# Softplus in an attention and dense-layer chain: where one plus the exponential is added

## The chip, the cores and the metric

The kernel runs on one core of a Trainium2 chip. The metric is the device time of one execution in microseconds (us). The engines are named as the profile names them: PE (TensorE, matmuls; PEld its weight loads), DVE (VectorE), ACT (ScalarE), POOL (GpSimd) and SP (SyncE, which issues most transfers).

## The reference

Windowed attention over q, k, v gives x of 1536 tokens by 512. A gated layer follows, then a layer with softplus:

```python
a = x @ w1
b = x @ w2
h = a * b @ w3
x = h @ w_out                                   # 1536 x 512
h = x @ w_in                                    # 1536 x 2048
g = np.maximum(h, 0.0) + np.log1p(np.exp(-np.abs(h)))
return g @ w_out2                               # 1536 x 512
```

`w_in` and the last `w_out` belong to the last dense part, in which the change lies. All values are float32.

## The kernel before

Every large matrix product is made with three matmuls: each operand is split into a high part and the remainder, a low part, and `mm3` (lines 164 to 168) adds high x high, high x low and low x high in PSUM. So each product of a 128x128 stationary block with a 128x512 moving block stands as three matmuls, at lines 166, 167 and 168.

The program goes through banded attention, two stages that make the gated products (`ab`) and the product of the two later weights (`w34`), a third that gives y, and then `stage4`, the last dense part (lines 724 to 783). It is built of 48 steps: three chunks t of 512 tokens, and in each 16 blocks f of 128 of the 2048 hidden columns.

- A step makes `h` of its block: 12 matmuls into one PSUM bank (tag S, 4 buffers).
- `softplus` (lines 688 to 722), a generator in three parts, turns `h` into `g`. Part one: the absolute value (L704, ACT), the exponential of its negative (L705, ACT) into tile `spa`, and one plus that into tile `spu` (L706, POOL). Part two: the logarithm of it into `spl` (L709, ACT), then three DVE operations (L711, L714, L717), of which the first two correct for the rounding of the sum and add the positive part of `h`. Part three: the high part `gh` (L720, ACT cast) and the low part `gl` (L151, DVE subtraction).
- `outs` adds `g` of a block times the output weights: 12 matmuls into four accumulators, `ox` and `o`, for four groups of 128 tokens. Here slices of `gh` and `gl` are the stationary operand.

The generator is driven so that `h` of a step is followed by part one of the same step, part three of the step before, then part two of the same step. `outs` runs two steps behind `h`. In the last two steps it is held back; then come the outputs of blocks 12, 13 and 14, and block 15 in pieces. The very last softplus works in two halves of 256 columns, into the tile `glast`, so that its first half can be used early.

For the first chunk a scheduler orders each engine's instructions from its own costs; for the other two the order is that of the code (`manual_schedule`). In the first chunk, at f = 3, 5, 7 and 9, `w4_unit` also decodes weight units 12 to 15, which arrive as 64-bit words. Each unit is two halves, and each half takes on ACT L193 and L196 (`dt`) and the cast to the high part `w4h` (L226), on DVE L201, L204, L210 and L215 and the subtraction for the low part `w4l` (L151). Units 0 to 11 were decoded earlier. Line 196 has a bias from a tile of one value per partition (`rebias`, line 912).

Of the kernel before, what the change touches and what calls it, by code (L numbers as in the profile page):

```python
# [9 lines left out]
F32 = mybir.dt.float32  # L10
# [6 lines left out]
ALU = mybir.AluOpType  # L17
AF = mybir.ActivationFunctionType
PSUM = bass.MemoryType.PSUM

P = 128
# [38 lines left out]
    P=(-697.11, -455.77, -631.6, -474.64, -647.58, -395.71), PV=(97.88, 94.31, 94.22, 97.88, 97.88, 169.98),  # L60
# [81 lines left out]
class Net:  # L142
# [545 lines left out]
    def softplus(self, pool, ps, f, t, parts=1):  # L688

        nc = self.nc  # L690

        def tl(n, dt=F32, nb=2):
            return pool.tile([P, CH], dt, tag=n, name=f"{n}{t}_{f}", bufs=nb)

        a, u, l = tl("spa"), tl("spu"), tl("spl")
        if (t, f) == (NCH - 1, NF2 - 1):

            g = self.slot(SLOT_AB, "glast")
            gh, gl = g[:, 0, :], g[:, 1, :]
        else:  # L700
            gh, gl = tl("gh", FR, 3), tl("gl", FR, 3)
        cuts = [slice(j * CH // parts, (j + 1) * CH // parts) for j in range(parts)]
        for c in cuts:
            nc.scalar.activation(a[:, c], ps[:, c], AF.Abs)  # L704
            nc.scalar.activation(a[:, c], a[:, c], AF.Exp, scale=-1.0)  # L705
            nc.gpsimd.tensor_scalar(out=u[:, c], in0=a[:, c], scalar1=1.0, scalar2=1.0, op0=ALU.add, op1=ALU.mult)  # L706
        yield
        for c in cuts:
            nc.scalar.activation(l[:, c], u[:, c], AF.Ln)  # L709

            nc.vector.scalar_tensor_tensor(  # L711
                out=u[:, c], in0=u[:, c], scalar=1.0, in1=a[:, c], op0=ALU.subtract, op1=ALU.subtract
            )
            nc.vector.scalar_tensor_tensor(  # L714
                out=u[:, c], in0=ps[:, c], scalar=0.0, in1=u[:, c], op0=ALU.max, op1=ALU.subtract
            )
            nc.vector.tensor_tensor(out=l[:, c], in0=l[:, c], in1=u[:, c], op=ALU.add)  # L717
        yield
        for c in cuts:
            self.last_hi = nc.scalar.copy(gh[:, c], l[:, c])  # L720
            self.lo_dve(gl[:, c], l[:, c], gh[:, c])
        yield gh, gl
# [184 lines left out]
    def run(self):  # L907
        tc, nc = self.tc, self.nc
        with tc.tile_pool(name="const", bufs=1) as const:
            self.flag = const.tile([P, 1], I32, name="flag")  # L910
            self.val = const.tile([P, 2], F32, name="val")
            self.rebias = const.tile([P, 1], F32, name="rebias")
            self.idle = const.tile([P, P], BF, name="idle")
            nc.vector.memset(self.idle, 0.0)
            nc.vector.memset(self.rebias, -8.0 * 16 * 896)
            nc.scalar.preload_act_table_set("natural_log_exp_and_others")
            self.bad = None
            self.net(True)
            with tc.If(self.bad != 0):
                self.net(False)  # L920
# [48 lines left out]
```

## Time and profile before

| | |
|---|---|
| runs of the kernel | 584.95 us median of 3 (584.88 to 585.05) |
| the profiled execution | 584.81 us, of which 582.9 us are its span |
| granted PE clock | 0.998 of full speed over the span |
| PE busy | 573.5 us, 98% |
| PE weight loads busy | 472.8 us, 81% |
| DVE busy | 431.0 us, 74% |
| ACT busy | 347.1 us, 60% |
| POOL busy | 82.4 us, 14% |

The span runs from the first to the last instruction that the profile records. Busy shares are means over stages with different limits: a share says what an engine does, not who waits for it. Matmuls overlap in the pipeline, so the distance between the starts of two of them, not the length of one, tells the pace of PE. In a timeline the bracket at a row's end is the engine's idle time ahead of that instruction and what ended it.

### The profile page before, as it was taken

How to read it: one execution, taken by the hardware profiler on the slowest of the kernel's cores; microseconds unless marked ns; L12 is line 12 of the kernel's file. 1: busy time of each engine (PE TensorE's matmuls, PEld its weight loads, DVE VectorE, ACT ScalarE, POOL GpSimd, SP SyncE). 2: the span in 40 equal slices, each digit the busy share in tenths (PEclk: the TensorE clock that was granted, in tenths of full speed). 3: DMA queues.
4: the chain of work that ended last, by engine and by line, in shares of the span. 5: the costliest groups of instructions: out<-in, count | busy, mean ns of one | idle time of the engine just before them, and what ended most of it. 6: DMA issues, size and time to landing. Idle time of an engine off the chain costs nothing.

```text
span 582.9 us, 9844 instructions
## 1 busy us (share of the span) xinstructions
PE 573.5 (98%) x3718; PEld 472.8 (81%) x3718; DVE 431.0 (74%) x906; ACT 347.1 (60%) x712; POOL 82.4 (14%) x162
## 2 busy tenths in 40 slices
PE   9999999999999999999999999999999999999996
PEld 6888788888888888888888777888888888888885
DVE  6889899999989976767988889845644554654553
ACT  7999967667566754545666668544444344444352
POOL 4657700000000000000000221111111011011010
PEclk9999999999999999999999999999999999999999
DMA  7566645454445523342643221000200000200002
GB/s 275 172 221 195 188 140 149 139 151 151 133 144 148 164 88 108 114 140 72 201 128 106 74 72 37 0 1 0 73 0 2 0 1 1 73 0 1 0 1 79
DMA packets 15512, 54.51 MB, mean 94 GB/s; under 512 B 1888, under 2 KB 1888, under 8 KB 15456
## 3 DMA queue, kind: packets, MB, share of 16 engines
q1 hardware_dynamic: 15168, 53.27, 29.3%
q8 instruction: 31, 0.51, 0.4%
q10 hardware_dynamic: 288, 0.52, 0.3%
q14 instruction: 25, 0.20, 0.1%
HBM read 50.64 MB, written 3.15 MB: 92 GB/s over the span
## 4 chain that ended last, share of the span: by engine, by line
PE 86%; POOL 4%; DVE 3%; ACT 3%; issue 2%; DMA 1%; SPq 0%; POOLq 0%; DVEq 0%
PE ab L166 8%; PE ab L168 7%; PE ab L167 7%; PE h L167 6%; PE h L168 6%; PE h L166 6%; PE x2p L168 4%; PE x2p L166 4%; PE x2p L167 4%; PE ox L168 3%; PE o L167 3%; PE o L168 3%; PE o L166 3%; PE ox L167 3%; PE ox L166 3%; PE w34p L168 2%
## 5 line engine op out<-in xcount | busy, mean ns | idle before, releaser
L706 POOL TENSOR_SCALAR spu<-spa 128x512 f32<-128x512 f32 (+1 forms) x49 | 35.9, 733 | 458.7 <-ACT spa L705 458.7
L151 DVE TENSOR_TENSOR gl<-spl,gh 128x512 fp32r<-128x512 f32 x47 | 32.6, 694 | 76.8 <-ACT gh L720 76.5
L704 ACT ACTIVATE spa<-h 128x512 f32<-128x512 f32 (+1 forms) x49 | 28.7, 586 | 86.5 <-PE h L168 86.3
L166 PE MATMUL ab<-x,u_w 128*128 128x512 f32 x192 | 74.8, 390 | 0.0
L167 PE MATMUL ab<-x,u_w 128*128 128x512 f32 x192 | 74.7, 389 | 0.0
L168 PE MATMUL ab<-x,u_w 128*128 128x512 f32 x192 | 74.7, 389 | 0.0
L166 PE MATMUL h<-y,w4h 128*128 128x512 f32 x192 | 74.7, 389 | 0.0
L167 PE MATMUL h<-y,w4h 128*128 128x512 f32 x192 | 74.7, 389 | 0.0
L168 PE MATMUL h<-y,w4l 128*128 128x512 f32 x192 | 74.7, 389 | 0.0
L193 ACT ACTIVATE dt_w<-raw_w 128x512 bf16<-128x512 bf16 x64 | 42.5, 669 | 52.1 <-DMA raw_w<-w4d 16.9
L201 DVE SCALAR_TENSOR_TENSOR dc_w<-raw_w,dt_w 128x512 uint16<-128x512 uint16 x64 | 44.2, 697 | 10.1 <-ACT dt_w L196 9.6
L196 ACT ACTIVATE dt_w<-dt_w,rebias 128x512 uint16<-128x512 uint16 x64 | 45.8, 721 | 1.3
L711 DVE SCALAR_TENSOR_TENSOR spu<-spu,spa 128x512 f32<-128x512 f32 (+1 forms) x49 | 33.3, 680 | 16.6 <-ACT spl L709 16.6
L709 ACT ACTIVATE spl<-spu 128x512 f32<-128x512 f32 (+1 forms) x49 | 30.4, 623 | 24.5 <-POOL spu L706 24.5
L407 POOL TENSOR_SCALAR e<-e,st 128x196 f32<-128x196 f32 (+1 forms) x96 | 39.5, 434 | 23.4 <-ACT e L393 17.1
L393 ACT ACTIVATE e<-e,st 128x196 f32<-128x196 f32 (+1 forms) x96 | 42.2, 447 | 0.9 <-DVE st L386 0.7
L168 PEld LDWEIGHTS ab<-x,u_w 128*128 128x128 f32 x192 | 36.1, 188 | 7.5
L167 PEld LDWEIGHTS h<-y,w4h 128*128 128x128 f32 x192 | 36.1, 188 | 7.5
L167 PEld LDWEIGHTS ab<-x,u_w 128*128 128x128 f32 x192 | 36.0, 188 | 7.5
L166 PEld LDWEIGHTS h<-y,w4h 128*128 128x128 f32 x192 | 36.0, 188 | 7.5
L166 PEld LDWEIGHTS ab<-x,u_w 128*128 128x128 f32 x192 | 36.0, 188 | 7.4
L168 PEld LDWEIGHTS h<-y,w4l 128*128 128x128 f32 x192 | 36.0, 188 | 7.4
(127 smaller groups left out, 1306.4 us busy)
## 6 DMA issues: line engine op xcount, KB each, us to landing
raw_w<-w4d SPq DMA_DIRECT2D x32, 511.8 KB, 4.2
raw_w<-w SPq DMA_DIRECT2D x16, 511.8 KB, 4.6
raw_w<-w3t SPq DMA_DIRECT2D x16, 511.8 KB, 3.8
qk<-qk SPq DMA_DIRECT2D x7, 792.0 KB, 4.5
raw_wo<-wod SPq DMA_DIRECT2D x8, 511.8 KB, 3.8
v<-vu SPq DMA_DIRECT2D x8, 400.0 KB, 5.5
v<-v SPq DMA_DIRECT2D x8, 384.0 KB, 4.6
out<-os SPq DMA_DIRECT2D x10, 256.0 KB, 2.3
```

Of the source, the lines that this page charges most:

```text
L151: return engine.tensor_tensor(out=lo, in0=x, in1=hi.bitcast(F32), op=ALU.subtract)
L166: nc.tensor.matmul(ps, lhs[0], rhs[0], start=start, stop=False)
L167: nc.tensor.matmul(ps, lhs[0], rhs[1], start=False, stop=False)
L168: nc.tensor.matmul(ps, lhs[1], rhs[0], start=False, stop=stop)
L193: return nc.scalar.activation(t.bitcast(BF), x["top"].bitcast(BF), AF.Abs)
L196: return nc.scalar.activation(x["t"], x["t"], AF.Relu, bias=self.rebias[:, 0:1], scale=8.0)
L201: nc.vector.scalar_tensor_tensor(out=c, in0=x["top"], scalar=0x8000, in1=t, op0=ALU.bitwise_and, op1=ALU.bitwise_or)
L393: nc.scalar.activation(e, e, AF.Exp, bias=st[:, 0, i : i + 1], scale=-1.0, accum_out=st[:, 1, i : i + 1])
L407: nc.gpsimd.tensor_scalar(out=e, in0=e, scalar1=buf("st", h)[:, 2, i : i + 1], scalar2=1.0, op0=ALU.mult, op1=ALU.mult)
L706: nc.gpsimd.tensor_scalar(out=u[:, c], in0=a[:, c], scalar1=1.0, scalar2=1.0, op0=ALU.add, op1=ALU.mult)
L709: nc.scalar.activation(l[:, c], u[:, c], AF.Ln)
L711: nc.vector.scalar_tensor_tensor(out=u[:, c], in0=u[:, c], scalar=1.0, in1=a[:, c], op0=ALU.subtract, op1=ALU.subtract)
```

## The change

The addition at L706 is made by ACT, as an Identity activation whose bias is a tile that holds one, in all 49 places (47 steps of 512 columns, and the two halves of 256 of the last step). The tile `one` is added and filled by DVE at the start.

```diff
         for c in cuts:
             nc.scalar.activation(a[:, c], ps[:, c], AF.Abs)
             nc.scalar.activation(a[:, c], a[:, c], AF.Exp, scale=-1.0)
-            nc.gpsimd.tensor_scalar(out=u[:, c], in0=a[:, c], scalar1=1.0, scalar2=1.0, op0=ALU.add, op1=ALU.mult)
+            nc.scalar.activation(u[:, c], a[:, c], AF.Identity, bias=self.one[:, 0:1])
...
             self.rebias = const.tile([P, 1], F32, name="rebias")
+            self.one = const.tile([P, 1], F32, name="one")
             self.idle = const.tile([P, P], BF, name="idle")
             nc.vector.memset(self.idle, 0.0)
             nc.vector.memset(self.rebias, -8.0 * 16 * 896)
+            nc.vector.memset(self.one, 1.0)
```

The order of the built program moves in three places. The names carry the chunk and the step: `spa0_3` is tile `spa` of chunk 0, step 3; the last number is a running one.

ACT before, in chunk 0, from the second pass over weight unit 12 to the absolute value of step 4:

```order
L196 ACTIVATE dt_w4_12_1_3863<-dt_w4_12_1_3863,rebias_60 128x512 [waits Activation_49]
L720 CAST gh0_2_3819<-spl0_2_3818 128x512 [waits DVE_49]
L704 ACTIVATE spa0_3_3887<-h0_3_3874 128x512 [waits PE_49]
L705 ACTIVATE spa0_3_3887<-spa0_3_3887 128x512 [waits Activation_49]
L709 ACTIVATE spl0_3_3889<-spu0_3_3888 128x512 [waits Pool_49]
L226 CAST w4h12_3846<-dr_w4_12_0_3856 128x512 [waits DVE_49]
L226 CAST w4h12_3846<-dr_w4_12_1_3869 128x512 [waits DVE_49]
L704 ACTIVATE spa0_4_3926<-h0_4_3913 128x512 [waits PE_49]
```

The same place in the changed program:

```order
L196 ACTIVATE dt_w4_12_1_3865<-dt_w4_12_1_3865,rebias_60 128x512 [waits Activation_49]
L704 ACTIVATE spa0_3_3889<-h0_3_3876 128x512 [waits PE_49]
L720 CAST gh0_2_3821<-spl0_2_3820 128x512 [waits DVE_49]
L705 ACTIVATE spa0_3_3889<-spa0_3_3889 128x512 [waits Activation_49]
L706 ACTIVATE spu0_3_3890<-spa0_3_3889,one_61 128x512 [waits Activation_49]
L709 ACTIVATE spl0_3_3891<-spu0_3_3890 128x512 [waits Activation_49]
L226 CAST w4h12_3848<-dr_w4_12_0_3858 128x512 [waits DVE_49]
L226 CAST w4h12_3848<-dr_w4_12_1_3871 128x512 [waits DVE_49]
L704 ACTIVATE spa0_4_3928<-h0_4_3915 128x512 [waits PE_49]
```

The wait of the logarithm for POOL is gone, the Identity stands in its place, and the absolute value of step 3 has moved ahead of the cast of `gh` of step 2.

PE before, at the first output matmuls of the part (chunk 0, block 0):

```order
L166 MATMUL h0_3_3874<-y0_0_3216,w4h3_3340 128x512 [waits DVE_49]
L167 MATMUL h0_3_3874<-y0_0_3216,w4h3_3340 128x512
L166 MATMUL ox0_0_3830<-w4h0_3328,gh0_0_3767 128x512 [waits PE_49,Activation_49]
L167 MATMUL ox0_0_3830<-w4l0_3329,gh0_0_3767 128x512
L166 MATMUL ox0_1_3831<-w4h0_3328,gh0_0_3767 128x512 [waits PE_49]
L168 MATMUL ox0_0_3830<-w4h0_3328,gl0_0_3768 128x512 [waits DVE_49]
```

PE in the changed program, same place:

```order
L166 MATMUL h0_3_3876<-y0_0_3218,w4h3_3342 128x512 [waits DVE_49]
L167 MATMUL h0_3_3876<-y0_0_3218,w4h3_3342 128x512
L168 MATMUL h0_3_3876<-y0_0_3218,w4l3_3343 128x512
L166 MATMUL ox0_0_3832<-w4h0_3330,gh0_0_3769 128x512 [waits PE_49,Activation_49]
L167 MATMUL ox0_0_3832<-w4l0_3331,gh0_0_3769 128x512
L166 MATMUL ox0_1_3833<-w4h0_3330,gh0_0_3769 128x512 [waits PE_49]
L168 MATMUL ox0_0_3832<-w4h0_3330,gl0_0_3770 128x512 [waits DVE_49]
```

The third matmul of `h` of step 3 has moved from behind the 12 output matmuls to ahead of them.

ACT before, at the end of the part (chunk 2, steps 13 to 15):

```order
L720 CAST gh2_13_5656<-spl2_13_5655 128x512 [waits DVE_49]
L709 ACTIVATE spl2_14_5694<-spu2_14_5693 128x512 [waits Pool_49]
L704 ACTIVATE spa2_15_5719<-h2_15_5706 128x256 [waits PE_49]
L705 ACTIVATE spa2_15_5719<-spa2_15_5719 128x256 [waits Activation_49]
L704 ACTIVATE spa2_15_5719<-h2_15_5706 128x256
L705 ACTIVATE spa2_15_5719<-spa2_15_5719 128x256 [waits Activation_49]
L720 CAST gh2_14_5695<-spl2_14_5694 128x512 [waits DVE_49]
L709 ACTIVATE spl2_15_5721<-spu2_15_5720 128x256 [waits Pool_49] x2
```

And in the changed program:

```order
L706 ACTIVATE spu2_14_5695<-spa2_14_5694,one_61 128x512 [waits Activation_49]
L720 CAST gh2_13_5658<-spl2_13_5657 128x512 [waits DVE_49]
L709 ACTIVATE spl2_14_5696<-spu2_14_5695 128x512 [waits Activation_49]
L704 ACTIVATE spa2_15_5721<-h2_15_5708 128x256 [waits PE_49]
L705 ACTIVATE spa2_15_5721<-spa2_15_5721 128x256 [waits Activation_49]
L706 ACTIVATE spu2_15_5722<-spa2_15_5721,one_61 128x256 [waits Activation_49]
L704 ACTIVATE spa2_15_5721<-h2_15_5708 128x256
L705 ACTIVATE spa2_15_5721<-spa2_15_5721 128x256 [waits Activation_49]
L706 ACTIVATE spu2_15_5722<-spa2_15_5721,one_61 128x256 [waits Activation_49]
L720 CAST gh2_14_5697<-spl2_14_5696 128x512 [waits DVE_49]
L709 ACTIVATE spl2_15_5723<-spu2_15_5722 128x256
```

Three Identity activations now stand on ACT ahead of the cast of `gh` of step 14, where POOL did that work beside it. The order on DVE and SP is unchanged, but for the added fill at the start.

## Rows read from the trace of the kernel before

**Rows 1.** Busy time by stretch (window, engine busy us and count, clock, DMA, GB/s).
```profile
340.00:362.00 22.00, 20.98 (x89) 16.12 (x88) 19.98 (x35) 14.90 (x27) 5.33 (x4) 1.00 0.21 73
```

**Rows 2.** Timeline of PE: start, length, instruction; first, 232nd, last matmul of the part.
```profile
313.57 0.39 PE L166 MATMUL h<-y,w4h 128*128 128x512 f32 x1
...
368.69 0.39 PE L166 MATMUL ox<-w4h,gh 128*128 128x512 f32 x1
...
577.22 0.39 PE L168 MATMUL o<-w4h,glast 128*128 128x512 f32 x1
```

**Rows 3.** Waits of weight loads from 313 us (total, times, longest); the first one's timeline row.
```profile
PEld ox L168 <- DVE gl L151: 2.4, 5, 1.0
...
322.42 0.19 PEld L166 LDWEIGHTS ox<-w4h,gh 128*128 128x128 f32 x1 [0.50 <-ACT gh L720]
```

**Rows 4.** Timeline of ACT, POOL and DVE, chunk 0, steps 3 and 5.
```profile
328.82 0.63 ACT L705 ACTIVATE spa<-spa 128x512 f32<-128x512 f32 x1
329.53 3.12 POOL L706 TENSOR_SCALAR spu<-spa 128x512 f32<-128x512 f32 x1 [5.30 <-ACT spa L705]
331.48 0.69 DVE L151 TENSOR_TENSOR gl<-spl,gh 128x512 fp32r<-128x512 f32 x1
332.69 0.63 ACT L709 ACTIVATE spl<-spu 128x512 f32<-128x512 f32 x1 [3.24 <-POOL spu L706]
333.86 1.29 DVE L151 TENSOR_TENSOR w4l<-dr_w,w4h 128x512 fp32r<-128x512 f32 x2 [1.69 <-ACT w4h L226]
...
341.96 3.05 POOL L706 TENSOR_SCALAR spu<-spa 128x512 f32<-128x512 f32 x1 [5.72 <-ACT spa L705]
```

**Rows 5.** Instructions that write tile spu: ns minimum, median, maximum; first and last start.
```profile
L706 POOL TENSOR_SCALAR spu<-spa x49: 403/617/3122, 317.8 to 568.4; 128x512 f32<-128x512 f32 x47, 128x256 f32<-128x256 f32 x2
```

**Rows 6.** Timeline of DVE: one operation of the decode of units 13, 14 and 15.
```profile
341.04 0.29 DVE L204 TENSOR_SCALAR dt_w<-dc_w 128x512 uint16<-128x512 uint16 x1
...
353.39 0.29 DVE L204 TENSOR_SCALAR dt_w<-dc_w 128x512 uint16<-128x512 uint16 x1
...
364.38 0.29 DVE L204 TENSOR_SCALAR dt_w<-dc_w 128x512 uint16<-128x512 uint16 x1
```

**Rows 7.** ACT by line and shape: count, busy us, mean ns, idle ahead and its releasers.
```profile
L196 ACT ACTIVATE dt_w<-dt_w,rebias 128x512 uint16<-128x512 uint16 x64 | 45.8, 721 | 1.3
L193 ACT ACTIVATE dt_w<-raw_w 128x512 bf16<-128x512 bf16 x64 | 42.5, 669 | 52.1 <-DMA raw_w<-w4d 16.9 <-DVE dr_w L210 11.3 <-DMA raw_w<-w3t 6.3
...
L709 ACT ACTIVATE spl<-spu 128x512 f32<-128x512 f32 x47 | 29.7, 632 | 24.5 <-POOL spu L706 24.5
L705 ACT ACTIVATE spa<-spa 128x512 f32<-128x512 f32 x47 | 29.7, 632 | 1.5
L720 ACT CAST gh<-spl 128x512 fp32r<-128x512 f32 x47 | 28.6, 608 | 12.8 <-DVE spl L717 12.8
L704 ACT ACTIVATE spa<-h 128x512 f32<-128x512 f32 x47 | 28.0, 595 | 86.4 <-PE h L168 86.3
...
L226 ACT CAST w4h<-dr_w 128x512 fp32r<-128x512 f32 x8 | 4.7, 614 | 1.0 <-DVE dr_w L215 1.0
...
L705 ACT ACTIVATE spa<-spa 128x256 f32<-128x256 f32 x2 | 0.8, 418 | 0.1
```

**Rows 8.** Timeline, chunk 2: low part of step 13, and the first matmul that uses step 13.
```profile
565.85 0.69 DVE L151 TENSOR_TENSOR gl<-spl,gh 128x512 fp32r<-128x512 f32 x1 [2.44 <-ACT gh L720]
...
569.29 0.39 PE L166 MATMUL ox<-w4h,gh 128*128 128x512 f32 x1
```

**Rows 9.** Timeline of the tail: ACT, DVE, and the weight load for the first low part.
```profile
568.88 0.62 ACT L720 CAST gh<-spl 128x512 fp32r<-128x512 f32 x1 [0.56 <-DVE spl L717]
569.41 0.72 ACT L709 ACTIVATE spl<-spu 128x256 f32<-128x256 f32 x2
...
572.73 0.42 DVE L151 TENSOR_TENSOR glast<-spl,glast 128x256 fp32r<-128x256 f32 x1
...
573.60 0.19 PEld L168 LDWEIGHTS ox<-w4h,glast 128*128 128x128 f32 x1
```

## The prediction

> **What bounds the kernel now.** I began with the busy time by stretch [rows 1]: between 340 and 362 us TensorE (PE) is busy for 20.98 us of 22, VectorE (DVE) for 19.98, ScalarE (ACT) for 14.90 and GpSimd (POOL) for 5.33. PE is the bound almost everywhere, so only a hole in PE's stream can give time back. The next view is the timeline of PE [rows 2]. The last dense part runs 48 steps of 12 matmuls `h` and 12 matmuls of the output, 1152 in all. The first starts at 313.57, the 232nd at 368.69, the last at 577.22. The last 920 pitches take 208.53 us, 0.2267 us each, with no room for a wait of visible size. The 231 pitches ahead would take 52.37 us at that pace and take 55.12. So **2.75 us** is lost in the whole part, all of it between 313.57 and 368.69, while the last four weight units (12 to 15) are decoded beside the first chunk's steps.
>
> Who made PE wait stands in the waits of its weight loads [rows 3], since here `gh` and `gl` are the stationary operands: `gl` from DVE five times. The first wait of all, at 322.42, is for the first `gh` from ACT; with the short stumbles behind it (up to 323.80, where the 44th matmul would have stood at 323.32) it costs 0.48 us. The other 2.27 us come from 344 us on. There I read ACT, DVE and POOL against each other [rows 4]: the POOL operation of step 3 starts at 329.53 and lasts 3.12 us. The exponential ahead of it ended at 329.45 (328.82 + 0.63). The logarithm behind it (L709) starts at 332.69, after ACT sat idle for 3.24 us. ACT's two casts of weight unit 12 are queued behind that logarithm, and DVE, done with `gl` at 332.17, waits 1.69 us for them and starts its subtraction only at 333.86. At 341.96 the same happens with 3.05 us. The median L706 is 617 ns, the longest 3122 [rows 5]. DVE's own start-to-start distance between decodes shows the effect [rows 6]: 12.35 us from unit 13 to unit 14 (353.39 − 341.04), 10.99 to unit 15 (364.38 − 353.39), against 48 x 0.2267 = 10.88 us that PE needs for two steps. The holes of PE are that delay, arriving a few steps later.
>
> A long POOL span may be an artefact. **A rule against my reading:** the Trainium skill, Perfetto Trace Analysis, GPSIMD Engine Instruction, says that GpSimd spans in a profile are unreliable and should be timed by what follows them. If the 3.12 us were only recorded, nothing would be saved. Here what follows confirms it: L709 starts 0.04 us after the recorded end [rows 4].
>
> **The change, step by step.** 49 POOL operations go, 49 Identity activations with a per-partition bias come, 47 of 128x512 and two of 128x256. The trace shows no Identity. Below I bound it with the exponential and the logarithm of the same shape, 632 ns; above with the activation at L196, which also has a bias tile, 721 ns. I take 0.72, as the bias operand makes L196 the nearest row, and the half-size one as 0.42 + 0.09 = 0.51 [rows 7]. A dependent ACT operation starts some 0.03 us after the end of the one ahead of it (0.04 behind POOL, [rows 4]); an independent one 0.09 before it, as the logarithms at 569.41 behind the cast that ends at 569.50 [rows 9].
>
> *Ordinary steps.* Before, exponential to logarithm took 0.08 + 0.62 + 0.04 us over POOL [rows 4, 5]; now it is 0.03 + 0.72 + 0.03 on ACT: 0.04 more. In the first chunk ACT had nothing queued between the two, so its idle time is filled and nothing is pushed back by more than that.
>
> *Decode steps, the gain.* Behind the exponential that ends at 329.45 the Identity ends about 330.2, the logarithm about 330.9 instead of 333.32. Now DVE comes last: its `gl` start at 331.48 shows the second sum done about 331.55 [rows 4], so the casts run 331.0 to 332.2 and the subtraction starts about 332.1, right behind `gl`, instead of 333.86. That is 1.75 us per long operation, so the two of them give back 3.5 us on DVE's queue, more than PE lost. What DVE still has to do for two steps is below 10.99 us, and that figure holds a DVE operation which POOL delayed; so its `gl` stays ahead of PE, by my walk about 1.1 us ahead at steps 4 and 6. ACT's work for two steps plus a unit is 2 x (0.595 + 0.632 + 0.632 + 0.608) + 2 x (0.669 + 0.721 + 0.614) = 8.94 us [rows 7]; with two Identities 10.38, still under 10.88. The 2.27 us go.
>
> *The moved matmul.* In the new order one more matmul of step 3 stands ahead of the first output matmul. `gh` comes at the same time, so it fills one pitch of the first wait: 0.23 of its 0.48 us, leaving 0.25. ACT also starts the absolute value of step 3 ahead of the cast of `gh` 2; DVE reads that cast only at 331.48, so this costs nothing.
>
> *Chunks 1 and 2.* There the cast of `gh` of the step before stands behind the Identity and moves back by 0.75 us. `gl` of step 13 ends at 566.54; the third matmul of its outputs, which start at 569.29, needs it at about 569.5 [rows 8]. The cover of 2.95 us shrinks to 2.2: free. Without it every microsecond beyond would be paid in each of 32 steps.
>
> *The tail, a cost.* Three Identities now stand on ACT ahead of the cast of the last-but-one `gh` (step 14). Walking that queue: Identity 14 delays the cast of `gh` 13 by 0.75 and the logarithm of 14 by 0.42, so the first half's absolute value starts about 566.99; then two halves of absolute value, exponential and Identity, 566.99 + 0.41 + 0.45 + 0.42 + 0.40 + 0.45 + 0.41 = 569.53, against 568.88 [rows 9]. All behind it is one chain of ACT and DVE, so the first `glast` subtraction ends at 573.15 + 0.65 = 573.80. PE loads that operand at 573.60; 0.05 us of signalling makes it 573.85. A load this late costs its lateness less what a matmul stands ahead of its use, here about **0.13 us** (bounds: 0 with Identity at 0.632, 0.4 if nothing overlaps).
>
> The added tile and its fill on DVE at the start lie before the first data arrive: nothing.
>
> **Sum.** 2.75 − 0.25 − 0.13 = 2.37 us less. The profiled execution's own time is 584.81, 0.14 below the median of 584.95; 584.95 − 2.37 = **582.6**.
>
> **Rivals.** (a) *DVE paces the decode anyway.* It is busy for 91% of 340 to 362 [rows 1]. If part of the 12.35 us is its own and the cycle falls only to 11.6, three cycles lose 3 x 0.72 = 2.2 us, less the 1.1 ahead: 1.1 us of holes stay, 583.7. Against it: the 1.69 us wait of [rows 4] and the 10.99 of a cycle without a long POOL operation. Chance 0.12, most of it still faster.
>
> (b) *The delay is hidden or not real*: the logarithm waits as long for something else, such as DVE's release of a buffer, and the holes stay: 584.9. This is also what the rule on GpSimd spans would give. The 3.24 us that ended 0.04 us after POOL's end speak against it: 0.08.
>
> (c) *ACT becomes the pace, slower.* Place: the decode cycles. From (10.88 − 8.94) / 2 = 0.97 us per Identity on, ACT decides. At 1.44, twice my row, four cycles lose 4 x 0.94 − 1.1 = 2.7 us, and the tail's shift becomes 0.65 + 0.72 + 2 x 0.51 = 2.4 us, of which some 1.9 reach PE: 584.95 − 2.75 + 0.25 + 2.7 + 1.9 = 587.0. Against it: no activation of this shape in [rows 7] is above 0.73, and the built program holds no second table load. Chance 0.05. The Trainium skill, ScalarE: Activation LUTs, Rules for kernel authors, speaks for this side: it puts an add on VectorE rather than ScalarE. By that rule alone 49 x (0.72 − 0.62) = 4.9 us are added to the work; [rows 2] show that after 368.69 none of it meets a waiting PE.
>
> That the change does not do what it says is excluded by the order of the built program.
>
> **How the numbers follow.** Forecast 0.75, spread 582.1 (no hole left, noise of 0.1) to 583.2 (Identity and cover off by the bounds); (a) 0.12, (b) 0.08, (c) 0.05. The range 582.1 to 583.8 takes in the forecast and most of (a). About 0.2% (1.17 us) is what a measurement can tell from no change. Faster: 0.75 + 0.09 = 0.84; same: 0.03 + 0.08 = 0.11; slower 0.05.
>
> **What would show it.** Right: Identity near 0.72 us; no idle of ACT above 1 us ahead of the logarithm between 325 and 345; `gl` no longer a releaser of PE from 344 us on; the last matmul about 2.4 us earlier; one short late load near the first `glast` subtraction. Wrong: waits of PE for `gl` in the decode steps that stay (a, b), ACT without gaps there (c), or more than 0.5 us of PE waiting in the tail.

## The result and the profile after

The changed kernel takes **592.95 us** (median of 4 runs, 592.79 to 593.7) against 584.91 (4 runs of the kernel before, 584.63 to 585.05) on the same chip: a ratio of **1.014 [1.0123, 1.0158]**. The forecast was 582.6. The profiled execution takes 593.09 us, 590.9 of them span, at a granted clock of 0.999; the kernel before had 584.81, 582.9 and 0.998. The clock is not the reason.

Busy time of the changed kernel, from the page:

```profile
PE 582.0 (99%) x3718; PEld 473.7 (80%) x3718; DVE 426.7 (72%) x907; ACT 379.7 (64%) x761; POOL 46.3 (8%) x113
```

36 us have left POOL and 33 have come to ACT. But PE, which issues the same 3718 matmuls, is busy for 8.5 us more. The stretch in which the gain was forecast, and a later one, by window (columns as in [rows 1]):

```profile
340.00:362.00 22.00, 22.00 (x97) 17.97 (x96) 20.78 (x37) 19.28 (x33) 0.00 (x0) 1.00 0.25 85
...
400.00:480.00 80.00, 80.00 (x349) 65.08 (x348) 38.85 (x59) 45.06 (x77) 0.00 (x0) 1.00 0.04 14
```

and the later one in the kernel before:

```profile
400.00:480.00 80.00, 80.00 (x355) 66.26 (x354) 42.09 (x62) 36.53 (x62) 9.26 (x15) 1.00 0.04 14
```

Between 340 and 362 PE has no hole left: 97 matmuls against 89 [rows 1]. (The last part starts 6 us later in the changed kernel, so a window holds slightly earlier steps of it.) Between 400 and 480, where PE is busy throughout in both kernels, 349 matmuls run, and 355 in the kernel before. So PE is not waiting more, it has become slower. Four matmuls date the places: the first of the gated products (`ab`), the first behind the 768 matmuls of `ab` and `w34`, the first `h` of the last part, and the last of all. After:

```profile
74.99 0.50 PE L166 MATMUL ab<-x,u_w 128*128 128x512 f32 x1
...
254.30 0.39 PE L166 MATMUL x2p<-ab,w 128*128 128x512 f32 x1
...
319.58 0.39 PE L166 MATMUL h<-y,w4h 128*128 128x512 f32 x1
...
584.69 0.39 PE L168 MATMUL o<-w4h,glast 128*128 128x512 f32 x1
```

Before (the other two stand in [rows 2], 313.57 and 577.22):

```profile
74.08 0.50 PE L166 MATMUL ab<-x,u_w 128*128 128x512 f32 x1
...
248.29 0.39 PE L166 MATMUL x2p<-ab,w 128*128 128x512 f32 x1
```

| stretch | before, us | after, us | difference |
|---|---|---|---|
| up to the first `ab` | 74.08 | 74.99 | +0.91 |
| `ab` and `w34`, 768 matmuls | 174.21 | 179.31 | **+5.10** |
| x2p (the stage that gives y) | 65.28 | 65.28 | 0.00 |
| the last part | 263.65 | 265.11 | **+1.46** |

That makes 7.47 at the last matmul. The largest share arises in a stage in which no instruction was changed. There the pitch of PE goes from 174.21 / 768 = 0.2268 us to 179.31 / 768 = 0.2335, while x2p right behind it keeps its pace. Some 0.5 us more lies behind the last matmul; that stretch lasts 5.68 us in this profile of the kernel before (582.9 − 577.22), 6.21 after, and 6.39 in a second profile of the kernel before, so I make nothing of it.

The matmuls by tile tell which are slower (ns minimum, median, maximum; first and last start). After:

```profile
L166 PE MATMUL ab<-x,u_w x192: 392/396/503, 75.0 to 253.6; 128*128 128x512 f32 x192
...
L166 PE MATMUL x2p<-ab,w x96: 388/389/390, 254.3 to 318.9; 128*128 128x512 f32 x96
...
L166 PE MATMUL o<-w4h,gh x94: 392/396/398, 330.1 to 582.9; 128*128 128x512 f32 x94
...
L167 PE MATMUL o<-w4l,glast x2: 389/389/389, 583.8 to 584.5; 128*128 128x512 f32 x2
```

`ab` and the outputs that read `gh` last 396 ns; x2p and the outputs that read `glast` 389, though all have the same shape. What tells them apart is where their operands lie: the kernel allocates some tiles from the left end of SBUF (x, y, `ab`, the output weights, `glast`) and some from the right (the weight ring `u_w`, `gh`, `gl`). The slow ones take one operand from each side. The new tile `one` takes 32 bytes per partition on the left, ahead of all these, so every tile of the left side has moved up by 32 bytes; the right side has stayed. The traces do not show addresses; this follows from the order in which the kernel allocates, and the experiments put it to the test.

What the prediction spoke of on ACT and DVE did come. ACT's row of the new operation by shape, and step 3 on ACT and DVE:

```profile
L706 ACT ACTIVATE spu<-spa,one 128x512 f32<-128x512 f32 x47 | 34.0, 723 | 1.5
...
L706 ACT ACTIVATE spu<-spa,one 128x256 f32<-128x256 f32 x2 | 1.0, 510 | 0.1
```

```profile
334.76 0.63 ACT L705 ACTIVATE spa<-spa 128x512 f32<-128x512 f32 x1
335.43 0.72 ACT L706 ACTIVATE spu<-spa,one 128x512 f32<-128x512 f32 x1
336.19 0.63 ACT L709 ACTIVATE spl<-spu 128x512 f32<-128x512 f32 x1
...
337.58 0.69 DVE L151 TENSOR_TENSOR gl<-spl,gh 128x512 fp32r<-128x512 f32 x1
338.18 1.29 DVE L151 TENSOR_TENSOR w4l<-dr_w,w4h 128x512 fp32r<-128x512 f32 x2
```

The exponential now hands over to the logarithm in 0.80 us (336.19 − 334.76 − 0.63) where it took 3.24 [rows 4], and DVE's subtraction for `w4l` stands right behind `gl`. DVE's cycle is regular, 10.98 and 11.04 us, where one of 12.35 stood before [rows 6]:

```profile
334.77 0.49 DVE L204 TENSOR_SCALAR dt_w<-dc_w 128x512 uint16<-128x512 uint16 x2
...
345.75 0.49 DVE L204 TENSOR_SCALAR dt_w<-dc_w 128x512 uint16<-128x512 uint16 x2
...
356.79 0.49 DVE L204 TENSOR_SCALAR dt_w<-dc_w 128x512 uint16<-128x512 uint16 x2
```

The waits of the weight loads from 313 us on (total, times, longest) are 1.0 us in all, against 3.7 before: 2.4 for `gl` [rows 3], and 1.3 for `gh` from ACT, of which [rows 3] have only the first 0.5:

```profile
PEld ox L166 <- ACT gh L720: 1.3, 2, 0.8
```

After:

```profile
PEld ox L166 <- DVE os L741: 0.4, 2, 0.2
PEld ox L166 <- ACT gh L720: 0.3, 1, 0.3
PEld ox L168 <- DVE gl L151: 0.3, 1, 0.3
```

### The profile page after: what moved, and what is told of

Same layout as the page of the kernel before. It is cut to its first block, busy times and chain, and to the rows that moved or that the text cites. A ratio compares the mean times of both kernels' runs of the same rounds, so it can differ in the third digit from the quotient of the medians.

```text
span 590.9 us, 9800 instructions
## 1 busy us (share of the span) xinstructions
PE 582.0 (99%) x3718; PEld 473.7 (80%) x3718; DVE 426.7 (72%) x907; ACT 379.7 (64%) x761; POOL 46.3 (8%) x113
## 4 chain that ended last, share of the span: by engine, by line
PE 92%; POOL 3%; ACT 3%; DMA 1%; DVE 1%; issue 0%; SPq 0%; POOLq 0%; DVEq 0%
PE ab L166 8%; PE ab L167 8%; PE ab L168 8%; PE h L168 7%; PE h L166 7%; PE h L167 7%; PE ox L166 4%; PE ox L168 4%; PE ox L167 4%; PE o L166 4%; PE o L167 4%; PE o L168 4%; PE x2p L166 4%; PE x2p L167 4%; PE x2p L168 4%; POOL e L407 3%
## 5 line engine op out<-in xcount | busy, mean ns | idle before, releaser
L166 PE MATMUL ab<-x,u_w 128*128 128x512 f32 x192 | 76.0, 396 | 0.0
L167 PE MATMUL ab<-x,u_w 128*128 128x512 f32 x192 | 75.9, 395 | 0.0
L168 PE MATMUL ab<-x,u_w 128*128 128x512 f32 x192 | 75.9, 395 | 0.0
L168 PE MATMUL x2p<-ab,w 128*128 128x512 f32 x96 | 37.4, 389 | 0.0
L166 PE MATMUL x2p<-ab,w 128*128 128x512 f32 x96 | 37.4, 389 | 0.0
```

The costliest lines, as they stand in the source:

```text
L166: nc.tensor.matmul(ps, lhs[0], rhs[0], start=start, stop=False)
L167: nc.tensor.matmul(ps, lhs[0], rhs[1], start=False, stop=False)
L168: nc.tensor.matmul(ps, lhs[1], rhs[0], start=False, stop=stop)
```

## The experiments

### Is it the work or the place?

Theory P: the place of the tiles makes matmuls slow. W: the added work of ACT does. L: the left side's own address does. One kernel makes the change without moving an address: `rebias`, which uses 4 of its 32 bytes, gets a second column that holds one.

```diff
-            nc.scalar.activation(u[:, c], a[:, c], AF.Identity, bias=self.one[:, 0:1])
+            nc.scalar.activation(u[:, c], a[:, c], AF.Identity, bias=self.rebias[:, 1:2])
...
-            self.rebias = const.tile([P, 1], F32, name="rebias")
-            self.one = const.tile([P, 1], F32, name="one")
+            self.rebias = const.tile([P, 2], F32, name="rebias")
```

> The whole change, but the value one lies in a second column of the tile rebias, so that no tile's address moves. Theory P (placement: a matmul whose stationary and moving operand lie at different offsets within 64 bytes takes 0.2333 us instead of 0.2267): the pitch of ab, w34p and the outputs is back at 0.2267, the waits of PE from 344 us on stay away, 582.6 us. Theory W (the work: 49 more ACT instructions slow the matmuls beside them, through SBUF or instruction supply): nothing changes against the change, 592.9 us. Theory L (the left tiles' own address, multiples of 64, is slow whatever the other operand): 582.6 us as P.

The second is the kernel before with POOL's add as it was and an unused tile on the left:

```diff
             self.rebias = const.tile([P, 1], F32, name="rebias")
+            self.pad = const.tile([P, 1], F32, name="pad")
```

> The kernel before, with an unused tile of one value per partition that moves the left tiles by 32 bytes; POOL still adds. P: 768 matmuls of ab and w34p at +0.0066 us and 564 of the outputs at +0.0070 us, 5.1 + 3.9 = 9.0 us, and the 0.9 us by which the changed kernel's attention ended later if that has the same cause: 593.9 to 594.8 us. W: 584.9 us. L: 593.9 us as P.

The third adds to the changed kernel an unused tile at the right end, the fourth adds that tile to the kernel before:

```diff
+        low = sb("low", "right")
+        nc = self.nc
+        nc.vector.memset(low.tile([P, 1], F32, name="pad_right"), 1.0)
         self.dec = sb("dec", "right")
```

> The change as it is, and the right tiles moved by 32 bytes too, so that left and right have the same offset within 64 bytes again (both a multiple of 64). P: 582.6 us, pitch of ab, w34p and outputs 0.2267. W: 592.9 us. L: 592.9 us.

> The kernel before with the right tiles alone moved by 32 bytes; the left ones lie as before, POOL still adds. P: as with the left ones moved, 593.9 to 594.8 us. W: 584.9 us. L: 584.9 us.

| kernel | left, right moved by | median, us | ratio to before | `ab` and `w34`, us |
|---|---|---|---|---|
| change, one in `rebias` | 0, 0 | 584.35 | 0.9998 [0.9981, 1.0015] | 174.21 |
| before, left tile | 32, 0 | 594.12 | 1.0146 [1.0114, 1.0179] | 179.30 |
| change, right tile | 32, 32 down | 587.10 | 1.0038 [1.0021, 1.0055] | 175.91 |
| before, right tile | 0, 32 down | 593.78 | 1.0146 [1.0121, 1.0171] | 179.30 |

The kernel before had 585.21 beside these. A ratio is worked out from all runs of both kernels, so it is not exactly the quotient of two medians. The timelines of PE that give the last column, for the right tile in the kernel before:

```profile
77.20 0.50 PE L166 MATMUL ab<-x,u_w 128*128 128x512 f32 x1
...
256.50 0.39 PE L166 MATMUL x2p<-ab,w 128*128 128x512 f32 x1
```

and in the changed kernel:

```profile
75.44 0.50 PE L166 MATMUL ab<-x,u_w 128*128 128x512 f32 x1
...
251.35 0.39 PE L166 MATMUL x2p<-ab,w 128*128 128x512 f32 x1
```

It is the place, and W falls: the change without the move costs nothing that these runs can tell, and an unused tile alone, on either side, costs 1.4 to 1.5%, with the same 179.30 us in `ab` and `w34` as the change. L falls too, as the fourth kernel is slow with its left side where it was. But P as it was worded, the same offset within 64 bytes, does not hold either: the third kernel was to come back to 582.6 us and 174.21, and with left and right moved towards each other its pitch is 0.2290. So it isn't the address of one side.

### Which distances are slow?

Theory D: the distance between the two operands of a matmul decides. M: the offset within 64 bytes does, and a left tile at a multiple of 64 is a little slow by itself. The kernel before with a larger left tile of 64 bytes (`[P, 16]`) and of 128 (`[P, 32]`), and the changed kernel with 480 bytes more (`[P, 120]`), so that its left side stands 512 higher than before:

> The kernel before with its left tiles moved by 64 bytes. Theory D (what counts is the distance between stationary and moving operand, and 64 bytes off is not as good as 0): pitch of ab, w34p and outputs 0.2289 as with both sides moved by 32, some 588 us. Theory M (only the offset within 64 bytes counts, and a left tile at a multiple of 64 is a little slow by itself): pitch 0.2267, 584.9 us.

> The kernel before with its left tiles moved by 128 bytes. Theory D with a period of 128 bytes: pitch 0.2267, 584.9 us. Theory D with a longer period, or with a cost that grows with any distance: pitch above 0.2267 in ab, w34p and the outputs. Theory M: 0.2267.

> The change as it is, with one more unused tile so that the left tiles move by 512 bytes instead of 32. Theory D with a period of 512 bytes or a divisor of it: pitch 0.2267 in ab, w34p and the outputs, and the time of the kernel with one in rebias (584.4 us on the two chips seen). If any shift costs: above 590 us.

And one kernel of matmuls alone, which leaves the whole computation of the reference out. It shifts a stationary tile by s and a moving tile by m bytes from places of the same remainder, and issues 48 matmuls of the kernel's shape for each pair:

```diff
+            for s in STATIONARY:
+                for m in MOVING:
...
+                    x = [low[:, m // 4 + j * CH : m // 4 + (j + 1) * CH] for j in range(2)]
```

> Nothing of the reference is computed here: only matmuls of the kernel's kind (128x128 by 128x512, pairs of high and low operands in the order of mm3), 48 at a time, with the stationary operand moved by 0, 32, 64, 96, 128 or 256 bytes and the moving one by 0 to 480 in steps of 32, from tiles that both lie 480 bytes past a multiple of 512, as in the kernel before. Theory D (the distance between the operands counts): 0.2267 us for equal shifts, about 0.2333 where they differ by 32, 0.2289 at 64, and the same time along each diagonal. Theory A (each operand's own address counts): rows or columns, not diagonals. Theory O (it takes the other engines' traffic): 0.2267 us everywhere.

The two smaller shifts have one execution each. 64 bytes: 586.58 us, `ab` and `w34` in 175.92, a pitch of 0.2291, that of the third kernel above, which has the same change of distance by another road. 128 bytes: 593.41 us and 178.57, a pitch of 0.2325. So M falls. 512 bytes: 585.49 us, ratio 1.0019 [1.0006, 1.0032]; `ab` and `w34` 174.90, with the old pitch of 0.2267 and two waits for late weights, 0.7 and 0.2 us.

The timeline of the matmuls alone, with the stationary tile shifted by 32 bytes (second letter b); the third letter is the shift of the moving tile, b = 32, c = 64, up to k = 320. The start of a row less that of the row above, by 48, is the pitch of the row above:

```profile
202.18 11.05 PE L48 MATMUL qbb<-moving,stationary 128*128 128x512 f32 x48
213.06 11.37 PE L48 MATMUL qbc<-moving,stationary 128*128 128x512 f32 x48
224.27 11.16 PE L48 MATMUL qbd<-moving,stationary 128*128 128x512 f32 x48
235.26 11.37 PE L48 MATMUL qbe<-moving,stationary 128*128 128x512 f32 x48
246.47 11.36 PE L48 MATMUL qbf<-moving,stationary 128*128 128x512 f32 x48
257.67 11.40 PE L48 MATMUL qbg<-moving,stationary 128*128 128x512 f32 x48
268.92 11.35 PE L48 MATMUL qbh<-moving,stationary 128*128 128x512 f32 x48
280.11 11.35 PE L48 MATMUL qbi<-moving,stationary 128*128 128x512 f32 x48
291.30 11.05 PE L48 MATMUL qbj<-moving,stationary 128*128 128x512 f32 x48
302.18 11.37 PE L48 MATMUL qbk<-moving,stationary 128*128 128x512 f32 x48
```

`qbb`, both shifted by 32, takes (213.06 − 202.18) / 48 = 0.2267 us; `qbj`, moving at 288 against 32, the same again. `qbd` (a distance of 64) takes 0.2290, the rest 0.2331 to 0.2344. Over the 96 pairs, without the first, which meets PE's start-up, and the last, whose end cannot be read, the pitch follows the moving address less the stationary one alone, and repeats after 256 bytes. The table has the median for each distance, from the unrounded starts; the pairs of one distance lie within 0.5 ns of each other:

| distance, bytes | 0 | 32 | 64 | 96 | 128 | 160 | 192 | 224 |
|---|---|---|---|---|---|---|---|---|
| ns per matmul | 226.8 | 233.4 | 229.1 | 233.6 | 233.3 | 234.2 | 233.2 | 233.1 |

So D, with a period of 256 bytes, when matmuls run alone. x is the moving operand and the ring's tile the stationary one; in the kernel before both lie 480 bytes past a multiple of 512, so their distance is a multiple of 256. The table gives 768 x (233.4 − 226.8) = 5.1 us for the shift by 32, as measured. The run with 128 bytes does not fit it: `ab` and `w34` have 0.2325 where the table has 0.2333, and `h` was slower too, 0.2298 in its steps instead of 0.2267 (the last part took 266.60 us), though both its operands had moved together. x2p, whose operands had moved together as well, kept its pace. So in that kernel something beside the distance counts, and what it is stays open.

### Was the 2.27 us there to be had?

In four of these kernels POOL still makes the add, and the number of its long L706 operations differs: the kernel before has three of them with the left tile of 32 bytes and none with 64, with 128 or with the right tile, two in [rows 4], with the same operations on both engines. So theory R: chance decides in each execution which of POOL and DVE goes first; against it F: the order of the program fixes it. The kernel before, unchanged, was profiled a second time:

> The kernel before, unchanged, for a second profile of it. Theory R (the long POOL additions are a matter of when they arrive beside DVE's decode operations, so their number differs from one execution to the next: 2 in the first profile, 3 and 0 in two copies whose tiles were only moved): another number of additions above 3 us, and a last part (first h to last matmul) shorter or longer by about 1 us for each. Theory F (they are fixed by the program): again two of 3.1 and 3.05 us, 263.65 us from the first h to the last matmul.

```profile
314.61 0.39 PE L166 MATMUL h<-y,w4h 128*128 128x512 f32 x1
...
330.11 1.70 DVE L210 SCALAR_TENSOR_TENSOR dr_w<-raw_w,dt_w 128x512 f32<-128x512 uint32 x2
330.56 0.72 POOL L706 TENSOR_SCALAR spu<-spa 128x512 f32<-128x512 f32 x1 [5.29 <-ACT spa L705]
...
576.01 0.39 PE L168 MATMUL o<-w4h,glast 128*128 128x512 f32 x1
```

and its row for that tile:

```profile
L706 POOL TENSOR_SCALAR spu<-spa x49: 406/620/720, 318.9 to 567.2; 128x512 f32<-128x512 f32 x47, 128x256 f32<-128x256 f32 x2
```

POOL starts 0.45 us behind DVE's pair of L210, as in the first profile (329.53 against this row of it):

```profile
329.08 1.28 DVE L210 SCALAR_TENSOR_TENSOR dr_w<-raw_w,dt_w 128x512 f32<-128x512 uint32 x2
```

but now DVE is the one delayed, 1.70 us for the pair instead of 1.28, and POOL takes 0.72 instead of 3.12. No L706 is above 0.72. The last part takes 576.01 − 314.61 = 261.40 us, **2.25 less** than the 263.65 from which I had worked. R holds against F: what the change was to give back is lost in some executions of the kernel before and not in others.

Both outcomes stand within the first profile too. Its second long operation (341.96, [rows 4]) and the one in the decode of unit 15, where DVE is delayed, both start 0.52 us behind the pair of L210:

```profile
341.44 1.29 DVE L210 SCALAR_TENSOR_TENSOR dr_w<-raw_w,dt_w 128x512 f32<-128x512 uint32 x2
...
353.79 1.70 DVE L210 SCALAR_TENSOR_TENSOR dr_w<-raw_w,dt_w 128x512 f32<-128x512 uint32 x2
354.31 0.64 POOL L706 TENSOR_SCALAR spu<-spa 128x512 f32<-128x512 f32 x1 [5.72 <-ACT spa L705]
```

So the chip alone does not settle it, and F falls by the second profile. What does settle it stays open: the two profiles do not tell whether they come from one chip, so a part of the chip in it, beside chance, is not excluded. The time of an execution does not show the outcome: the second profile's took 584.43 us, only 0.38 less than the first's, because `ab` and `w34` took 175.33 us there, with two waits of 0.7 for late weights, and the stretch behind the last matmul 0.71 more.

### What does the change cost where nothing moves?

The first kernel again, with more runs, and one in which ACT adds in the first chunk alone, where units are decoded; both have the one in `rebias`.

```diff
+            if t:
+                nc.gpsimd.tensor_scalar(out=u[:, c], in0=a[:, c], scalar1=1.0, scalar2=1.0, op0=ALU.add, op1=ALU.mult)
+            else:
+                nc.scalar.activation(u[:, c], a[:, c], AF.Identity, bias=self.rebias[:, 1:2])
```

> The same kernel as in the run with one in rebias, for a narrower interval. In that run the last matmul started 1.95 us earlier than in the kernel before; if that is what a whole execution gains, 583.0 us, a ratio of 0.9967. Rival (the end of the program gives it back): a ratio of 1.000.

> ACT adds in the first chunk's 16 steps only, POOL as before in the other two chunks; the value one lies in the tile rebias, so no address moves. Theory P with my prediction's mechanism (the gain is the decode steps of the first chunk; the cost is the two chunk boundaries, where DVE's copies of the accumulators come late, and the tail): last matmul 2.4 to 2.5 us earlier than in the kernel before, no late weight load at the boundaries or in the tail, 582.5 us. Rival (part of the gain comes from POOL being idle in the later chunks): the last matmul at most as early as in the run with one in rebias, 1.95 us ahead of the kernel before.

> The kernel with ACT adding in the first chunk alone, timed once more. If theory R holds, what it saves depends on the executions of the kernel before that it is measured against: where those have long POOL additions (as on the chip of the first profile, 263.65 us from the first h to the last matmul), a ratio near 0.996; where they have none (261.40 us in the second profile), 0.9996, no difference. Its own last part is 261.2 us either way. If the delay in the kernel before were fixed, 0.996 each time.

| ACT adds | median, us | before, us | ratio | last part, us |
|---|---|---|---|---|
| everywhere (first runs) | 584.35 | 585.21 | 0.9998 [0.9981, 1.0015] | 261.71 |
| everywhere (again) | 584.54 | 583.57 | 1.0019 [1.0002, 1.0037] | 261.72 |
| in the first chunk | 583.54 | 583.57 | 0.9997 [0.9982, 1.0012] | 261.22 |
| in the first chunk (again) | 583.72 | 584.07 | 0.9996 [0.9977, 1.0015] | 261.22 |

Against the 261.40 of the undisturbed kernel before, the change loses 0.3 us in the last part and the version for the first chunk gains 0.2. The waits of the weight loads from 313 us on, for ACT everywhere:

```profile
PEld ox L166 <- DVE os L741: 0.6, 2, 0.3
PEld ox L166 <- ACT gh L720: 0.3, 1, 0.3
PEld ox L168 <- DVE gl L151: 0.3, 1, 0.3
PEld ox L168 <- DVE glast L151: 0.3, 1, 0.3
```

and for ACT in the first chunk (its cast stands three lines further down):

```profile
PEld ox L166 <- ACT gh L723: 0.3, 1, 0.3
PEld ox L168 <- DVE gl L151: 0.3, 1, 0.3
```

The first row is new: DVE's copy of the accumulators at a chunk's end (L741) comes later and holds up the first output of the next chunk, twice. No version shown here beats the kernel before by what a measurement can tell: the ratios of 0.9967 and 0.996 and the 582.5 us that the expectations name for a gain did not come. The version for the first chunk equals the kernel before both times. ACT everywhere is 0.2% slower in its second set of runs, and 1 lies just outside that interval.

## Why the prediction was wrong

- **The step that failed:** "The added tile and its fill on DVE at the start lie before the first data arrive: nothing." The fill costs nothing (the kernel with the one in `rebias` has a second fill as well, and its `ab` starts at 74.07); the tile's 32 bytes cost 5.10 us in `ab` and `w34` and, against the same change without a move, 265.11 − 261.71 = 3.40 in the last part, 8.50 together. I priced the tile as an instruction and not as a shift of every tile allocated behind it. No rival had this mechanism. The two addresses stood in the built program before the run; what the trace of before could not show is that their distance matters.
- **"The 2.27 us go"**: right in mechanism, wrong as a gain. `gl` waits from 344 us on are gone, the logarithm waits for no one, and with the move taken away DVE's cycle is 10.9, which is PE's own for two steps. With the move taken away the last part is 263.65 − 261.71 = 1.94 us shorter than in the profile I read, where I had forecast 2.37. But the second profile of the kernel before is 2.25 shorter by itself. I took a loss seen in one execution for a property of the kernel, and that this execution stood 0.14 us from the median does not tell the two apart.
- **"The holes of PE are that delay"**: shown, since they are absent where no L706 is long. One of them, 0.8 us at 349.49, was a wait for `gh` from ACT, not for `gl`; it is gone with the others. The rule of the Trainium skill, Perfetto Trace Analysis, GPSIMD Engine Instruction, that GpSimd spans are unreliable does not bear here: the long span was real, and did not come back in the second profile. What does bear is the Trainium skill, SBUF — State Buffer, Who interferes with whom: a VectorE instruction with two inputs in SBUF and a GpSimd instruction that reads SBUF want the same port pair, and whichever issues first keeps the other out. The two outcomes of one meeting, POOL held for 3.12 us or DVE delayed by 0.42, agree with it. Which of the two comes first at 0.45 us behind L210 no run here explains.
- **The Identity:** forecast 0.72 and 0.51, measured 0.723 and 0.510. **ACT as the pace** (rival c) and **DVE as the pace** (rival a) did not come: with the move taken away, no weight load waits between 330 and 368 us, where the units are decoded. Rival (b), no gain, comes closest to what the change without the move is worth, though for another reason than it gave: not that the stall stays, but that it is not in every execution. **The moved matmul:** the first wait is 0.3 instead of 0.5, near the forecast.
- **"The cover of 2.95 us shrinks to 2.2: free"**: true of `gl`, for which no load waits behind 330 us. Missed were the two boundaries between chunks, where a weight load waits 0.3 us. What the first of them costs on PE, in the second profile with ACT everywhere:

```profile
409.95 0.39 PE L168 MATMUL ox<-w4h,gl 128*128 128x512 f32 x1
...
410.55 0.39 PE L167 MATMUL ox<-w4l,gh 128*128 128x512 f32 x1
```

These two starts are two pitches apart: 0.60 us instead of 0.45. The second boundary takes the same (497.16 to 497.76), so the two cost 0.3. With 0.2 less at the first wait and 0.1 more in the tail that makes +0.2, against 261.72 − 261.40 = 0.32 measured; the other 0.1 has no row.

- **The tail:** one late load for `glast`, 0.3 us long, as forecast; PE's starts around it, 572.16 and 572.50, are 0.34 us apart, 0.11 more than a pitch, where 0.13 was forecast.
- **The sum as it was:** +0.91 until `ab`, +5.10, 0.00, and +3.40 − 1.94 in the last part. The +0.91 is not explained: `ab` starts at 74.00 to 76.78 in versions with nothing moved and at 74.73 to 77.20 in shifted ones, so the place of tiles may have no part in it.

## What to carry to other kernels

Before pricing the work of an edit, look at what it does to addresses: a tile of one value per partition, allocated early, moves all behind it, and for fp32r matmuls of 128x512 the distance between the moving and the stationary operand should stay a multiple of 256 bytes (2.9% of PE's pitch here). That held in all kernels here but one, so the pitch is read again after the edit. Where a constant is wanted, a spare column of a tile that exists moves nothing. And a stall that comes of two engines meeting is profiled twice before its removal is booked as a gain.

## What the runs showed of the hardware

- In the kernel of matmuls alone the pitch of a 128x512 matmul depends on the distance of its two operands in SBUF modulo 256 bytes: 226.8 ns at 0, 229.1 at 64, 233.1 to 234.2 elsewhere, not symmetric (64 against 192), at a granted clock of 0.997. The other kernels agree but for the one with 128 bytes, whose `h` took 229.8 at an unchanged distance. The Trainium skill, SBUF — State Buffer, Who interferes with whom, states that PE waits for no other engine at its ports; these runs don't speak against that, since in the matmuls alone no other engine works beside PE, and the loss is between PE's own two operands.
- A POOL operation of 0.62 us that meets DVE's stream of two-operand instructions is held through several of them, back to back, until that stream ends (3.12 us), or else delays one of them (0.42 us), at the same arrival: 0.45 us behind the stream's L210 in two executions of one program, 0.52 us twice in one execution. In six profiles with POOL at work there, two have held operations and four none.
